# Moving 97 subtractions of a two-layer kernel from VectorE to GpSimd

## The chip, the core and the metric

The kernel runs on one core of one Trainium2 chip. The metric is the device time of the program in microseconds (us); less is better. Engines are named as the profile names them: PE is the matrix engine (TensorE), DVE the vector engine (VectorE), ACT the scalar engine (ScalarE), POOL is GpSimd, SP issues the DMA transfers. PSUM is the memory that PE writes its sums to, SBUF the working memory.

## What is computed

A chunked attention with 8 memory slots feeds two dense layers. Only the first dense layer (`_moe_ref`) matters for the change.

```python
out[:, :, c_start:c_end] = np.matmul(a, v_full)        # softmax attention, 32 queries per chunk
...
x = attention output, 3072 tokens x 512
h = np.maximum(x @ w_in, 0.0)                          # layer 1: 512 -> 2048
x = (h * h @ w_out)                                    # layer 1: 2048 -> 512
...
h = x @ w2_in                                          # layer 2
g = np.maximum(h, 0.0) + np.log1p(np.exp(-np.abs(h)))  # softplus
return (g @ w2_out)
```

The kernel keeps float32 accuracy on PE by splitting each operand into a high half, which is the value rounded to the matrix engine's format, and a low half, which is the value less its high half. A product of two such operands takes three matmuls: high by low, low by high, high by high.

## The kernel before

The 3072 tokens of layer 1 are six blocks (n = 0 to 5) of 512 tokens; a block runs 16 steps (f = 0 to 15), one for each slice of 128 of the 2048 hidden units. A step is, in PE's order:

- `h_mm(1, n, f)` (L286): 12 matmuls of 128x512 that make `hp`, one slice of x @ w_in, from the block's halves `xh`, `xl` and the weight halves `wt[1, f]`.
- `act1` (L302), on ACT: Relu into a tile `r` (L304), Square in place (L305), and a copy to `gh`, the high half (L307). It notes (gl, r, gh) in the list `rest`.
- `act1_low` (L311): takes the oldest entry of `rest` and issues gl = r - gh (L313), the low half. This is the line that the change touches.
- `out_step` (L359) with `out_mm` (L319): 12 matmuls that add gh and gl times the second weights into four PSUM banks `acc`. It stays `LOOK` = 2 steps behind `h_mm`, so PE works on other slices between the making of gh, gl and their use.

The tiles `r`, `gh` and `gl` have three buffers each. Everything up to the end of layer 1 stands under a manual schedule: each engine takes its instructions in the order in which the code issues them, and only semaphores hold them up. In the second layer only PE's order is written by hand.

Block 0 also prepares layer 1's weights. They come as 64-bit numbers by DMA, and for each slice `i` a job makes the two float32 halves: `w_a` (L98, ACT) takes the absolute value, `w_b` (L102, DVE, one input, in place) prepares the low bits, `w_d` (L107 and L110, DVE, two inputs each) joins them, `w_h` (L118, ACT) copies the high half, `w_p` (L122, DVE) subtracts for the low half. `h_mm(1, 0, f)` needs slice f's result, and `out_mm` that of its OUT part. In step f of block 0 the job of slice f + 2 runs (slice halves IN and OUT apart in the first steps), and around it the code issues:

```python
w_d(1, i, m)
w_h(1, i, m)
if k == 0:
    act1_low()
if flat:
    w_a(1, *flat[0])
    w_b(1, *flat[0])
w_p(1, i, m)
```

So DVE's queue in a step of block 0 reads L107, L110, L313, L102, L122. ACT's queue reads L304, L305, L307 (the step's `act1`), L118, then L98 of the next job. The softmax of the next block's attention stands in the same queues (`p_scores` on PE, `p_exp` and `p_norm` on DVE with L176 to L188, `p_transpose` on PE, `p_copy` on ACT at L218), and `pp` of `p_transpose` shares two PSUM buffers with `hp`. At the start of block 0 its first step is done in two halves of 256 tokens, so `rest` holds one entry more there, and L313 runs one step later than in the other blocks.

In blocks 1 to 5, `step` (L653) issues `act1_low` at the start of the step after the one that made gh. GpSimd has had six instructions in all, at the program's start.

Of the kernel before, what the change touches and what calls it, by code (L numbers as in the profile page):

```python
# [10 lines left out]
F32 = mybir.dt.float32  # L11
F32R = mybir.dt.float32r
AF = mybir.ActivationFunctionType
ALU = mybir.AluOpType
# [41 lines left out]
def body(ctx: ExitStack, tc: tile.TileContext, qk, vW, w1, w2, out):  # L56
    nc = tc.nc
# [252 lines left out]

    def act1_low():  # L311
        gl, r, gh = rest.pop(0)
        nc.vector.tensor_tensor(out=gl, in0=r, in1=gh.bitcast(F32), op=ALU.subtract)  # L313

    acc = [None] * 4
    rest = []
# [201 lines left out]
    with tc.manual_schedule(engines={mybir.EngineType.SP}):  # L518
# [20 lines left out]
        with tc.manual_schedule():  # L539
# [74 lines left out]
            for f in range(KF):  # L614
# [18 lines left out]
                for k, (i, m) in enumerate(jobs[f]):  # L633
                    flat.pop(0)
# [8 lines that stand above are left out]
                if not jobs[f]:  # L643
                    act1_low()
                if f % 4 == 0:
                    p_exp(pair)
                if f == KF - 1:
                    act1_low()
                    x_split((1, 1))
# [260 lines left out]
```

## Time and profile before

| | |
|---|---|
| time, median of 3 runs | 1107.55 us (1106.06 to 1107.64) |
| time of the profiled execution | 1106.41 us |
| its span, first to last instruction | 1104.6 us |
| PE busy | 1080.2 us, 98% |
| DVE busy | 753.2 us, 68% |
| ACT busy | 595.4 us, 54% |
| POOL busy | 0.7 us, 6 instructions |

The profiled execution lies 1.14 us under the median, and 1.81 us of its time are outside its span. PE is busy in nearly all of the span; an engine that is idle elsewhere costs nothing as long as PE doesn't wait for it. So the places to read are those in which PE waits, and what was late there.

### The profile page before, as it was taken

The numbers are of one execution on the slowest core, as the hardware profiler recorded it, in microseconds if no ns is written. First come the engines' busy times: TensorE is split into PE (matmuls) and PEld (weight loads), VectorE is DVE, ScalarE is ACT, GpSimd is POOL, SyncE is SP. The second block draws the span as 40 slices with busy tenths as digits, with TensorE's granted clock in tenths as the row PEclk, the third lists the DMA queues.
The fourth block names the chain that finished last, engine by engine and source line by source line (L and its number), as shares of the span: only waits on it lengthen the run. The fifth ranks groups of instructions, "written<-read, shape, count | busy, mean of one in ns | idle before, by whom it ended". The sixth has DMA issues, their size and how long they took to land.

```text
span 1104.6 us, 18583 instructions
## 1 busy us (share of the span) xinstructions
PE 1080.2 (98%) x7592; PEld 887.1 (80%) x7592; DVE 753.2 (68%) x1227; ACT 595.4 (54%) x926; POOL 0.7 (0%) x6
## 2 busy tenths in 40 slices
PE   6899999999999999999999999999999999999998
PEld 5678888888888888888888788888788888788886
DVE  6899586666668666777432798952798942798722
ACT  3676554454455445555544776632676632776522
POOL 0000000000000000000000000000000000000000
PEclk9899999999999999999999999999999999999999
DMA  9941253454525355442611755333555334555202
GB/s 368 408 178 45 64 166 121 150 187 154 187 88 204 105 176 177 161 153 110 225 39 64 262 186 222 117 141 137 203 188 217 111 136 147 196 200 191 77 1 76
DMA packets 49428, 174.99 MB, mean 158 GB/s; under 512 B 5312, under 2 KB 5312, under 8 KB 41152
## 3 DMA queue, kind: packets, MB, share of 16 engines
q1 hardware_dynamic: 49344, 173.82, 44.7%
q8 instruction: 59, 0.97, 0.3%
q14 instruction: 25, 0.20, 0.1%
HBM read 138.15 MB, written 35.65 MB: 157 GB/s over the span
## 4 chain that ended last, share of the span: by engine, by line
PE 91%; DVE 5%; ACT 2%; issue 1%; DMA 0%; SPq 0%; DVEq 0%
PE bk L830 23%; PE acc L328 23%; PE bk L742 18%; PE hp L292 8%; PE hp L293 7%; PE hp L294 7%; PE xs L237 1%; PE xs L156 1%; DVE cf L110 1%; DVE cf L107 1%; PE sc L156 1%; PE xp L237 1%; DVE h L753 1%; PE xpe L237 1%; ACT w L118 1%
## 5 line engine op out<-in xcount | busy, mean ns | idle before, releaser
L328 PE MATMUL acc<-gh,w 128*128 128x512 f32 (+1 forms) x776 | 238.9, 389 | 0.4 <-DVE w L122 0.4
L830 PE MATMUL bk<-ws,gh 128*128 128x512 f32 x768 | 236.6, 389 | 0.0
L742 PE MATMUL bk<-xo,ws 128*128 128x512 f32 x1008 | 231.1, 390 | 2.5 <-DVE h L791 2.5
L742 PEld LDWEIGHTS bk<-xo,ws 128*128 128x128 f32 x1008 | 188.7, 188 | 44.1 <-DVE h L791 5.1
L328 PEld LDWEIGHTS acc<-gh,w 128*128 128x128 f32 x776 | 144.0, 188 | 30.5 <-DVE w L122 0.8
L830 PEld LDWEIGHTS bk<-ws,gh 128*128 128x128 f32 x768 | 144.0, 188 | 30.1 <-ACT h L762 0.5
L292 PE MATMUL hp<-xh,w 128*128 128x512 f32 (+1 forms) x388 | 154.1, 397 | 3.5 <-ACT pt L218 3.1
L328 PE MATMUL acc<-gl,w 128*128 128x512 f32 (+1 forms) x388 | 150.5, 388 | 2.2 <-DVE gl L313 2.2
L294 PE MATMUL hp<-xh,w 128*128 128x512 f32 (+1 forms) x388 | 151.7, 391 | 0.0
L293 PE MATMUL hp<-xl,w 128*128 128x512 f32 (+1 forms) x388 | 151.6, 391 | 0.1
L830 PE MATMUL bk<-ws,gl 128*128 128x512 f32 x384 | 149.4, 389 | 0.0
L396 DVE TENSOR_TENSOR gl<-h,gh 128x512 fp32r<-128x512 f32 x96 | 66.0, 687 | 90.9 <-ACT gh L401 90.9
L401 ACT CAST gh<-h 128x512 fp32r<-128x512 f32 x96 | 59.3, 621 | 114.5 <-PE bk L830 114.2
L313 DVE TENSOR_TENSOR gl<-r,gh 128x512 fp32r<-128x512 f32 (+1 forms) x97 | 66.2, 683 | 73.0 <-ACT gh L307 72.6
L304 ACT ACTIVATE r<-hp 128x512 f32<-128x512 f32 (+1 forms) x97 | 57.2, 590 | 103.4 <-PE hp L294 99.7
L292 PEld LDWEIGHTS hp<-xh,w 128*128 128x128 f32 x388 | 73.9, 191 | 19.6 <-ACT pt L218 3.3
L328 PEld LDWEIGHTS acc<-gl,w 128*128 128x128 f32 x388 | 72.8, 188 | 17.7 <-DVE gl L313 2.9
L294 PEld LDWEIGHTS hp<-xh,w 128*128 128x128 f32 x388 | 73.8, 190 | 15.3
L293 PEld LDWEIGHTS hp<-xl,w 128*128 128x128 f32 x388 | 74.0, 191 | 14.8 <-DVE xl L282 0.3
L830 PEld LDWEIGHTS bk<-ws,gl 128*128 128x128 f32 x384 | 72.1, 188 | 15.1
L202 DVE STREAM_TRANSPOSE pt<-t 32x128 f32<-32x128 f32 x256 | 77.5, 303 | 4.3
L748 ACT ACTIVATE cf<-h 128x1024 f32<-128x1024 f32 x48 | 51.0, 1062 | 34.6 <-DVE cf L752 29.8
(81 smaller groups left out, 1139.8 us busy)
## 6 DMA issues: line engine op xcount, KB each, us to landing
ws<-wa SPq DMA_DIRECT2D x24, 1024.0 KB, 4.8
ws<-wo SPq DMA_DIRECT2D x24, 1024.0 KB, 4.8
ws<-wb SPq DMA_DIRECT2D x24, 768.0 KB, 4.3
r<-w SPq DMA_DIRECT2D x16, 1024.0 KB, 11.3
cf<-w SPq DMA_DIRECT2D x32, 512.0 KB, 5.3
qk<-qk SPq DMA_DIRECT2D x46, 336.0 KB, 5.1
v<-vW SPq DMA_DIRECT2D x44, 256.0 KB, 5.1
wo<-cf SPq DMA_DIRECT2D x16, 512.0 KB, 3.2
```

Of the source, the lines that this page charges most:

```text
L202: nc.vector.transpose(pt[b:b + 32, g], t[g * 32:(g + 1) * 32, i, h])
L292: nc.tensor.matmul(out=hp, lhsT=b, rhs=xh[:, c], start=(c == 0), stop=False)
L293: nc.tensor.matmul(out=hp, lhsT=a, rhs=xl[:, c], start=False, stop=False)
L294: nc.tensor.matmul(out=hp, lhsT=a, rhs=xh[:, c], start=False, stop=(c == KD - 1))
L304: nc.scalar.activation(out=r, in_=hp, func=AF.Relu)
L313: nc.vector.tensor_tensor(out=gl, in0=r, in1=gh.bitcast(F32), op=ALU.subtract)
L328: nc.tensor.matmul(out=acc[m][:, cols], lhsT=a, rhs=b, start=(f == 0 and j == 0 and cols.start == 0), stop=(f == KF - 1 and j == 2),)
L396: nc.vector.tensor_tensor(out=lo, in0=x, in1=hi.bitcast(F32), op=ALU.subtract)
L401: nc.scalar.copy(out=hi, in_=x)
L742: nc.tensor.matmul(out=bk, lhsT=a, rhs=b, start=(start and n == 0), stop=(n == 5), skip_group_check=not start)
L748: nc.scalar.activation(out=z, in_=h, func=AF.Abs)
L830: nc.tensor.matmul(out=bk, lhsT=a, rhs=b, start=(f == 0 and j == 0), stop=(f == KF - 1 and j == 2))
```

## The change

The subtraction of `act1_low` is issued on GpSimd's queue instead of VectorE's. Operands, tiles and its place in the code are the same.

```diff
     def act1_low():
         gl, r, gh = rest.pop(0)
-        nc.vector.tensor_tensor(out=gl, in0=r, in1=gh.bitcast(F32), op=ALU.subtract)
+        nc.gpsimd.tensor_tensor(out=gl, in0=r, in1=gh.bitcast(F32), op=ALU.subtract)
```

On DVE one instruction leaves each step. The piece below is step 2 of block 0, where the weight job of slice 4 runs (`r_4_334` is the raw slice, `w_4_741` its halves, `cf` the work tile).

```order
 L107 SCALAR_TENSOR_TENSOR cf<-cf,r_4_334 128x1024
 L110 SCALAR_TENSOR_TENSOR cf<-r_4_334,cf 128x1024
-L313 TENSOR_TENSOR gl<-r,gh 128x512
 L102 TENSOR_SCALAR r_2_186<-r_2_186 128x512
 L122 TENSOR_TENSOR w_4_741<-cf,w_4_741 128x1024
```

L102 and L122 now follow L110 directly; the other steps of layer 1 lose their L313 in the same way.

On POOL the 97 subtractions stand behind the making of the identity tile `ident`, with nothing between them. The piece is POOL's whole queue from there to the program's end.

```order
 masks.py:199 ISA
 masks.py:199 AFFINE_SELECT ident<-ident 128x128
+L313 TENSOR_TENSOR gl<-r,gh 128x256 x2
+L313 TENSOR_TENSOR gl<-r,gh 128x512 x95
 L906 UNCONDITIONAL_BRANCH
 L906 ISA
```

No other instruction shares that queue, so a subtraction can start as soon as its gh and a free gl are there.

On PE three matmuls move, where the last `out_mm` of layer 1 (`acc_5926` to `acc_5929`, slice 15) is interleaved with the first products of layer 2 (`bk`).

```order
 L328 MATMUL acc_5926<-gh,w_15_1480 128x512 x2
 L742 MATMUL bk<-xo_6081,ws 128x512
+L742 MATMUL bk<-xo_6083,ws 128x512 x3
 L328 MATMUL acc_5926<-gl,w_15_1480 128x512
 L328 MATMUL acc_5927<-gh,w_15_1480 128x512 x2
```

Three products of layer 2 now stand ahead of the first use of that slice's gl, three fewer behind the group. ACT's and SP's orders are the same.

## Rows read from the trace of the kernel before

**Rows 1.** The page: busy time, share of the span and instructions of each engine.

```profile
PE 1080.2 (98%) x7592; PEld 887.1 (80%) x7592; DVE 753.2 (68%) x1227; ACT 595.4 (54%) x926; POOL 0.7 (0%) x6
```

**Rows 2.** Windows: stretch, length, busy us: PE, PEld, DVE, ACT, POOL; clock, DMA.

```profile
30.00:72.00 42.00, 36.21 (x338) 28.40 (x337) 37.28 (x56) 26.03 (x41) 0.00 (x0) 0.92 0.90 355
72.00:125.00 53.00, 51.80 (x468) 42.13 (x469) 47.47 (x58) 37.83 (x53) 0.00 (x0) 1.00 0.18 57
...
154.00:250.00 96.00, 96.00 (x900) 78.59 (x900) 67.46 (x154) 48.47 (x87) 0.00 (x0) 1.00 0.45 153
```

**Rows 3.** PE's waits of the whole span: waiting line, releaser, us, times, longest.

```profile
PE hp L292 <- ACT pt L218: 3.1, 1, 3.1
```

**Rows 4.** The page's group of the moved line: instructions, busy us, mean ns, idle before.

```profile
L313 DVE TENSOR_TENSOR gl<-r,gh 128x512 fp32r<-128x512 f32 (+1 forms) x97 | 66.2, 683 | 73.0 <-ACT gh L307 72.6
```

**Rows 5.** Timeline of DVE, weight jobs in block 0: start, duration, instruction, [idle before].

```profile
40.85 0.42 DVE L313 TENSOR_TENSOR gl<-r,gh 128x256 fp32r<-128x256 f32 x1
41.19 0.42 DVE L102 TENSOR_SCALAR r<-r 128x512 uint32<-128x512 uint32 x1
41.62 0.69 DVE L122 TENSOR_TENSOR w<-cf,w 128x512 fp32r<-128x512 f32 x1
...
47.76 0.68 DVE L313 TENSOR_TENSOR gl<-r,gh 128x512 fp32r<-128x512 f32 x1
48.37 0.44 DVE L102 TENSOR_SCALAR r<-r 128x512 uint32<-128x512 uint32 x1
48.96 1.23 DVE L122 TENSOR_TENSOR w<-cf,w 128x1024 fp32r<-128x1024 f32 x1 [0.15 <-ACT w L118]
...
63.55 0.68 DVE L313 TENSOR_TENSOR gl<-r,gh 128x512 fp32r<-128x512 f32 x1
64.15 0.69 DVE L102 TENSOR_SCALAR r<-r 128x1024 uint32<-128x1024 uint32 x1
64.76 1.23 DVE L122 TENSOR_TENSOR w<-cf,w 128x1024 fp32r<-128x1024 f32 x1
...
73.67 1.22 DVE L122 TENSOR_TENSOR w<-cf,w 128x1024 fp32r<-128x1024 f32 x1
...
88.20 1.22 DVE L122 TENSOR_TENSOR w<-cf,w 128x1024 fp32r<-128x1024 f32 x1 [0.21 <-ACT w L118]
...
97.12 1.22 DVE L122 TENSOR_TENSOR w<-cf,w 128x1024 fp32r<-128x1024 f32 x1
...
112.75 1.22 DVE L122 TENSOR_TENSOR w<-cf,w 128x1024 fp32r<-128x1024 f32 x1 [1.32 <-ACT w L118]
...
121.38 1.22 DVE L122 TENSOR_TENSOR w<-cf,w 128x1024 fp32r<-128x1024 f32 x1 [0.52 <-ACT w L118]
```

**Rows 6.** Timeline of ACT, steps 1, 2 and 4 of block 0.

```profile
38.90 0.62 ACT L307 CAST gh<-r 128x512 fp32r<-128x512 f32 x1
40.97 0.62 ACT L118 CAST w<-cf 128x512 fp32r<-128x512 f32 x1 [1.45 <-DVE cf L110]
...
45.23 0.57 ACT L218 COPY pt<-pp 128x512 f32<-128x512 f32 x1
...
47.88 1.05 ACT L118 CAST w<-cf 128x1024 fp32r<-128x1024 f32 x1 [0.28 <-DVE cf L110]
...
63.67 1.06 ACT L118 CAST w<-cf 128x1024 fp32r<-128x1024 f32 x1 [0.75 <-DVE cf L110]
```

**Rows 7.** Timeline of PE: first gl of slice 4; first matmuls of h_mm 7, 11, 15.

```profile
73.20 0.51 PE L328 MATMUL acc<-gl,w 128*128 128x512 f32 x1 [1.82 <-DVE gl L313]
...
75.64 0.39 PE L292 MATMUL hp<-xh,w 128*128 128x512 f32 x1
...
100.20 0.39 PE L292 MATMUL hp<-xh,w 128*128 128x512 f32 x1
...
124.76 0.39 PE L292 MATMUL hp<-xh,w 128*128 128x512 f32 x1
```

**Rows 8.** Groups by line: the one instruction of POOL that reads SBUF.

```profile
masks.py:199 POOL TENSOR_SCALAR_AFFINE_SELECT ident<-ident 128x128 f32<-128x128 f32 x1 | 0.3, 292 | 0.1
```

## The prediction

> **What bounds the kernel now.** The page's busy times come first: PE is busy for 98% of the span, DVE for 68%, POOL for nothing [rows 1]. So nothing that only unloads DVE can help, except where PE waits for DVE. The windows show where that is. From 154 to 250 us PE is busy for all of its 96 us, while DVE has 28.5 us to spare. From 30 to 72 us PE is idle for 5.8 us and DVE is busy for 37.3 of 42 [rows 2]. That is block 0, where DVE and ACT make the weight halves. PE's waits name its longest hold there: 3.1 us for the copy pt (L218) on ACT [rows 3]. A second one, 1.82 us at 73.20, is for gl of slice 4, the very instruction that moves [rows 7]. So the timelines of DVE, ACT and PE in block 0 decide the case.
>
> What the reader is to see in DVE's timeline is what L122, the last instruction of a weight job, waits for. It needs L118 on ACT, and L118 needs DVE's L110. In step 2, L118 ends at 47.88 + 1.05 = 48.93 [rows 6] and L122 starts at 48.96; L313 and L102 lie in between, and 0.15 us are idle all the same [rows 5]. Step 1 ends L118 at 41.59 and starts L122 at 41.62, step 4 at 64.73 and 64.76 [rows 5, 6]. **L313 stands in the time that DVE spends on ACT's copy anyway.**
>
> **The change, part by part.** *What it removes.* 97 instructions of 683 ns, 66.2 us of DVE [rows 4]. In blocks 1 to 5 that is time which PE doesn't wait for: nothing. In block 0 each L313 is covered by L118, so L122 can't start sooner: nothing again. The pt copy stays too: it stands behind ACT's L118 and L98, which follow L110, not L313. What goes is the wait of 1.82 us, since POOL can make gl(4) right behind its gh instead of one job later. But what comes next is late as well. The weights of slice 7 are ready at 73.67 + 1.22 = 74.89 [rows 5], and h_mm(7), which needs them, starts at 75.64 [rows 7]. Of the 1.82 us only 0.75 can be had.
>
> *What it adds.* 97 instructions on POOL, alone in their queue, and a semaphore between POOL and PE in place of DVE's. ACT's `r` tiles are now freed by POOL; with three buffers that is no hold. The three matmuls that PE's order moves at the end of layer 1 are the same work: nothing.
>
> *How long one takes.* The trace has no two-input subtraction on POOL. The nearest row is a one-input one, 292 ns for 128 elements [rows 8]. Taking 0.1 us of that as fixed, 1.5 ns an element is left; 512 elements then take 0.87 us for one stream, and 1.64 us if the second stream costs as much again. My estimate lies between, 1.2 us. The Trainium skill (GPSIMD Engine Reference, 3.1 Elementwise — side-by-side cycle accounting) gives 4497 ns for 2048 elements; a quarter, 1.12 us, is an estimate from that page, and the sum below would be 0.9 us smaller by it.
>
> *What the overlap costs DVE.* The trace has no moment with both engines at work on SBUF, so this cost is bounded: nothing, or DVE stands still for POOL's whole instruction. A hint lies in the widths. The one-input L102 takes 0.69 us for 1024 elements, the two-input L122 takes 1.23 [rows 5]: a DVE instruction with two inputs uses all that DVE can read, one with one input reads at twice the pace and so uses it too. L107, L110, L102 and L122 are all of these kinds. If POOL reads through a path of DVE's, they and POOL exclude each other. I take that end as likelier, because these instructions leave no reading unused. The rule stands in the Trainium skill (SBUF — State Buffer, Who interferes with whom): a DVE instruction with two SBUF inputs, or in a two-port mode, and a GpSimd instruction that reads SBUF hold each other up until the first has finished. By that rule the time is the sum below, without it the first rival's 1106.85; no row here shows it.
>
> *The sum, if they exclude each other.* DVE runs L110 and L102 back to back, and POOL gets its turn in the pause ahead of L122. L102 issues where L313 did.
> - Step 1: gh is ready at 39.52 [rows 6]. L102 ends at 40.85 + 0.42 = 41.27, POOL at 42.47; L122 was at 41.62: **0.85 us** later.
> - Step 2: L102 ends at 48.20, POOL at 49.40, L122 was at 48.96: **0.44**. Step 3 has the same rows, with 0.03 more room: **0.4**.
> - Step 4: L102 is wide; it ends at 63.55 + 0.69 = 64.24, POOL at 65.44, L122 was at 64.76: **0.68**. Step 5 repeats this.
>
> Together 3.05 us. L122 feeds the next job's instructions, so the delay adds up. Slice 7's weights come at 74.89 + 3.05 = 77.94, and h_mm(7) starts then instead of at 75.64: PE is **2.3 us** late. Steps 6, 7 and 9 repeat step 4 (0.68 each); in step 8 L122 had waited 0.21 us for ACT, so 0.47. That makes 5.56 at L122 of slice 11: 97.12 + 1.22 + 5.56 = 103.90, where h_mm(11) was at 100.20 [rows 5, 7]: PE is now **3.7 us** late. Steps 10 and 11 add 0.68 each. Step 12 had 1.32 us of waiting for ACT, so it gives back 0.64; step 13 has no L102, and POOL's 1.2 us exceed L118's 1.06 by 0.14. The total is 6.42, and slice 15's weights come at 121.38 + 1.22 + 6.42 = 129.02, where h_mm(15) was at 124.76: **4.3 us** late at the end of block 0. From there PE has no wait to lose or win, and it keeps the 4.3 us to the end. The profiled execution of 1106.41 us becomes 1110.7; the median of the runs stands 1.14 us above it, so on that scale the forecast is 1111.8 us.
>
> With POOL at 0.87 us the same steps cost 0.52, 0.11, 0.07, 0.35, 0.35 and then 0.35 a step; slices 7, 11 and 15 then hold PE by some 0.7 us, 1108.3. With 1.64 us, 1.1 a step, it is some 10 us, 1117.5.
>
> **The rivals.**
>
> *No price for overlap* (chance 0.28). POOL and DVE read side by side. For it speaks that no row shows the opposite. Then gl(4) is early, h_mm(7) starts at 74.94, and PE gains 0.7 us: 1106.85. That is on the other side of before, by one mechanism, the wait at 73.20, and it decides wherever POOL costs DVE less than the room in front of L122 (0.35 us from 41.27, 0.76 us from 48.20). More than 2 us it can't give, since the wait itself has only 1.82.
>
> *Half a price* (0.10): POOL near 0.87 us, or a sharing that slows both a little. Some 0.7 us lost, 1108.3.
>
> *POOL is served first* (0.15). It takes its turn between L107 and L110 where gh is ready by then, in steps 1, 5, 9 and 13, and ahead of L102 elsewhere. A turn ahead of L110 costs the full 1.2 us, one ahead of L102 some 0.5 to 0.7. Slices 7, 11 and 15 then come 4.1, 7.2 and 8.9 us later, less the room of 0.75, 1.86 and 2.16 that PE had in front of them: 6.7 us lost, 1114.3.
>
> *POOL comes too late* (0.02). DVE's back-to-back work leaves it no turn, and PE waits for gl. Against it: gh(1) is ready at 39.52 and its gl was begun by DVE at 47.76 [rows 5, 6] without a hold of PE, so each POOL instruction has some 9 us. It decides only from there, and would cost several us a step.
>
> **How the numbers follow.** Forecast 0.45, the rivals 0.28, 0.10, 0.15 and 0.02. A difference of 0.2%, 2.2 us, is about what a measurement of this kernel can tell from no change. Slower by more: forecast, served first, too late, 0.62. Within: half a price and most of the first rival, 0.34. Faster by more: 0.04, the rest of the first rival, if something that I take as covered isn't. The likeliest time is 1111.8. The range goes down to the first rival's 1106.9 and up to 1115.5, past the served-first case; left out are the slowest POOL and a little below.
>
> **What would show it.** Right: POOL busy for some 1.2 us in each of 97 instructions, DVE's L122 in block 0 with waits on something that isn't ACT, or its instructions lengthened where POOL runs; h_mm(7) near 78, h_mm(11) near 104, h_mm(15) near 129 us, and no wait of PE for gl. Blocks 1 to 5 keep their length (PE 96 of 96 us), whatever DVE does. Wrong: DVE's instructions keep their 0.69 and 1.23 us beside a busy POOL and h_mm(7) starts at 75, or PE waits in blocks 1 to 5.

## Result, and the profile of the changed kernel

The changed kernel takes 1115.14 us (median of 6 runs, 1113.51 to 1116.75), the kernel before 1107.45 us (6 runs, 1106.06 to 1107.64). The ratio is 1.0070, with an interval of 1.0057 to 1.0083: 6.3 to 9.2 us slower. The forecast was 1111.8 us, slower, in a range of 1106.9 to 1115.5 us. The direction was right and the time lies in the range, near its upper end: a loss of 4.3 us was expected, and it is 7.7 us. The profiled execution of the changed kernel took 1115.76 us, with a span of 1114.0 us.

The page's busy times and its group of the moved line answer to [rows 1] and [rows 4]:

```profile
PE 1084.6 (97%) x7592; PEld 889.6 (80%) x7592; DVE 737.6 (66%) x1130; ACT 595.1 (53%) x926; POOL 132.6 (12%) x103
...
L313 POOL TENSOR_TENSOR gl<-r,gh 128x512 fp32r<-128x512 f32 (+1 forms) x97 | 131.9, 1359 | 478.1 <-ACT gh L307 443.5
```

DVE has lost 97 instructions, which took 66.2 us, but only 15.6 us of its busy time (753.2 to 737.6). So DVE's other instructions have become longer by some 50 us. That is the first sign of a price for the overlap.

The windows, with the stretches of [rows 2] and one more (stretch, length, busy us of PE, PEld, DVE, ACT, POOL; clock, DMA):

```profile
30.00:72.00 42.00, 35.49 (x337) 28.73 (x336) 35.93 (x46) 24.61 (x39) 7.25 (x5) 0.89 0.90 349
72.00:125.00 53.00, 49.30 (x449) 39.34 (x448) 48.63 (x50) 35.90 (x51) 14.20 (x8) 0.97 0.19 62
154.00:250.00 96.00, 96.00 (x900) 78.90 (x899) 62.90 (x137) 48.24 (x86) 20.90 (x16) 1.00 0.44 152
440.00:535.00 95.00, 93.32 (x822) 75.50 (x821) 60.61 (x118) 46.36 (x84) 19.67 (x16) 1.00 0.40 136
```

The last stretch in before:

```profile
440.00:535.00 95.00, 95.00 (x835) 78.28 (x834) 64.12 (x133) 50.69 (x91) 0.00 (x0) 1.00 0.46 153
```

PE now loses time in two places. One is block 0, as forecast. The other is at 440 to 535 us, where PE is busy for 93.32 of 95 us (in before for all 95); nothing was expected there. From 154 to 250 us it is busy for all of 96 us, as before.

PE's waits of the whole span (waiting line, releaser, us, times, longest), to be read beside [rows 3]:

```profile
PE hp L292 <- ACT pt L218: 7.2, 2, 4.7
...
PE hp L292 <- ACT xh L267: 0.7, 1, 0.7
PE acc L328 <- POOL gl L313: 0.7, 1, 0.7
```

The wait for pt was 3.1 us in one place and is 7.2 us in two. The wait of 1.82 us for gl(4) at 73.20 [rows 7] is gone. The waits for xh of L267 and for POOL's gl are new; both stand where block 4 ends.

In block 0, DVE's timeline in steps 1, 2 and 5 (start, duration, instruction, [idle before]) reads, to be set beside [rows 5]:

```profile
41.09 0.68 DVE L107 SCALAR_TENSOR_TENSOR cf<-cf,r 128x512 uint32<-128x512 uint32 x1
41.81 1.66 DVE L110 SCALAR_TENSOR_TENSOR cf<-r,cf 128x512 uint32<-128x512 uint32 x1
43.39 0.42 DVE L102 TENSOR_SCALAR r<-r 128x512 uint32<-128x512 uint32 x1
44.16 0.69 DVE L122 TENSOR_TENSOR w<-cf,w 128x512 fp32r<-128x512 f32 x1 [0.35 <-ACT w L118]
...
49.15 1.22 DVE L110 SCALAR_TENSOR_TENSOR cf<-r,cf 128x1024 uint32<-128x1024 uint32 x1
50.29 1.56 DVE L102 TENSOR_SCALAR r<-r 128x512 uint32<-128x512 uint32 x1
51.76 1.21 DVE L122 TENSOR_TENSOR w<-cf,w 128x1024 fp32r<-128x1024 f32 x1
...
74.81 2.21 DVE L110 SCALAR_TENSOR_TENSOR cf<-r,cf 128x1024 uint32<-128x1024 uint32 x1
76.94 0.68 DVE L102 TENSOR_SCALAR r<-r 128x1024 uint32<-128x1024 uint32 x1
78.13 1.23 DVE L122 TENSOR_TENSOR w<-cf,w 128x1024 fp32r<-128x1024 f32 x1 [0.51 <-ACT w L118]
```

In before, the L110 of step 1 reads:

```profile
40.24 0.69 DVE L110 SCALAR_TENSOR_TENSOR cf<-r,cf 128x512 uint32<-128x512 uint32 x1
```

POOL's timeline of the changed kernel in the same steps:

```profile
41.17 1.75 POOL L313 TENSOR_TENSOR gl<-r,gh 128x512 fp32r<-128x512 f32 x1 [7.12 <-ACT gh L307]
50.27 1.29 POOL L313 TENSOR_TENSOR gl<-r,gh 128x512 fp32r<-128x512 f32 x1 [7.35 <-ACT gh L307]
...
73.68 2.25 POOL L313 TENSOR_TENSOR gl<-r,gh 128x512 fp32r<-128x512 f32 x1 [5.89 <-ACT gh L307]
```

The timelines of the changed kernel are read together. In step 1 POOL's instruction is begun at 41.17, while DVE runs L107 until 41.77. DVE's L110 is begun at 41.81 and lasts 1.66 us in place of 0.69; POOL ends at 42.92, and L110 0.55 us behind that, at 43.47. So POOL waited for L107 to end, then ran for 1.15 us, and L110 stood still meanwhile. In step 2, L110 ends as POOL begins, POOL takes 1.29 us, and it is L102 that lasts 1.56 us instead of 0.44. Step 5 is like step 1, L110 lasting 2.21 us instead of 1.23. **In these steps POOL gets its turn as soon as the running DVE instruction ends**, ahead of the next one in DVE's queue.

PE's timeline: the first matmuls of h_mm 7, 11 and 15, to be set beside [rows 7]:

```profile
79.65 0.62 PE L292 MATMUL hp<-xh,w 128*128 128x512 f32 x1 [2.48 <-ACT pt L218]
...
105.97 0.40 PE L292 MATMUL hp<-xh,w 128*128 128x512 f32 x1
...
130.87 0.47 PE L292 MATMUL hp<-xh,w 128*128 128x512 f32 x1 [0.16 <-DVE w L122]
```

They stand 4.0, 5.8 and 6.1 us later than before. One caution on reading such a difference: TensorE's granted clock in block 0, as a mean over its levels of 2.4 GHz (1.00) and 1.2 GHz, is not the same in every execution. A kernel in which nothing of block 0 is changed (only one step of block 4, below) had its h_mm(7) at 79.92, with a granted clock of 0.71 from 25 to 32 us, where before had 1.00. So the sizes below come from medians of several runs wherever there are several, and single profiles are used for mechanisms and for stretches in which the clock is 1.00. The profile of before is also an early one: in the seven other profiles in which block 0 is as in before, h_mm(7) starts at 76.4 to 79.9 us and h_mm(15) at 126.0 to 129.1.

### The profile page after: what moved, and what is told of

The parts are those of the page before. It is cut to its first block, busy times and chain, and to the rows that moved or that the text cites. A ratio compares the mean times of both kernels' runs of the same rounds, so it can differ in the third digit from the quotient of the medians.

```text
span 1114.0 us, 18702 instructions
## 1 busy us (share of the span) xinstructions
PE 1084.6 (97%) x7592; PEld 889.6 (80%) x7592; DVE 737.6 (66%) x1130; ACT 595.1 (53%) x926; POOL 132.6 (12%) x103
## 4 chain that ended last, share of the span: by engine, by line
PE 49%; DVE 3%; ACT 1%; issue 0%; DVEq 0%
PE bk L830 23%; PE bk L742 18%; PE acc L328 4%; PE hp L294 1%; PE hp L293 1%; PE hp L292 1%; DVE h L753 1%; DVE cf L751 0%; DVE h L791 0%; DVE gl L396 0%; DVE cf L752 0%; ACT cf L749 0%; ACT cf L748 0%; ACT cf L750 0%; DVE xl L268 0%
## 5 line engine op out<-in xcount | busy, mean ns | idle before, releaser
L313 POOL TENSOR_TENSOR gl<-r,gh 128x512 fp32r<-128x512 f32 (+1 forms) x97 | 131.9, 1359 | 478.1 <-ACT gh L307 443.5
L396 DVE TENSOR_TENSOR gl<-h,gh 128x512 fp32r<-128x512 f32 x96 | 66.0, 688 | 90.7 <-ACT gh L401 90.7
L401 ACT CAST gh<-h 128x512 fp32r<-128x512 f32 x96 | 59.3, 621 | 114.2 <-PE bk L830 113.9
```

The lines of the kernel that those rows point to most:

```text
L313: nc.gpsimd.tensor_tensor(out=gl, in0=r, in1=gh.bitcast(F32), op=ALU.subtract)
L396: nc.vector.tensor_tensor(out=lo, in0=x, in1=hi.bitcast(F32), op=ALU.subtract)
L401: nc.scalar.copy(out=hi, in_=x)
```

## The experiments

Two theories stood against each other for the price: **exclusion** (POOL's reads and DVE's two-input or fast one-input instructions hold each other up) and **dependence** (PE waits for POOL's slower gl). Where the loss lies was open as well: in block 0 alone, or also in the blocks in which PE was never idle before. All kernels are made from the kernel before or after by the edit shown; `n` is the block, kept with the entry of `rest`. Their line numbers are one or two higher behind an added line (L313 may read L314).

### Block 0 and the others apart

```diff
-        nc.gpsimd.tensor_tensor(out=gl, in0=r, in1=gh.bitcast(F32), op=ALU.subtract)
+        engine = nc.gpsimd if n > 0 else nc.vector
+        engine.tensor_tensor(out=gl, in0=r, in1=gh.bitcast(F32), op=ALU.subtract)
```

> The subtraction is on GpSimd in blocks 1 to 5 only (80 of the 97); block 0 keeps it on VectorE. Theory (a GpSimd subtraction and VectorE's two-input instructions exclude each other, and it is block 0's weight jobs that pay for it): block 0 as before, h_mm of slice 7 at 75.6 and of slice 15 at 124.8 us; what is left is the cost of the late blocks, where the profile of the changed kernel lost 3.2 of its 9.35 us: 0 to 3 us over before. Rival (each subtraction is slow or late on GpSimd, and PE waits for gl): 80 of 97 instructions stay, so most of the loss stays, 6 us or more, with waits of PE for GpSimd in the trace.

Measured: 1111.84 us against 1108.0, a ratio of 1.0030 (1.0020 to 1.0039), 3.3 us slower, by the median a little above the expected 3. The second kernel has `n == 0` for the condition:

> The subtraction is on GpSimd in block 0 only (17 of the 97). Theory: 4 to 7 us over before, with L110 or L102 beside a GpSimd instruction 1 us longer than its 0.69 or 1.23 us, and h_mm of slice 15 some 6 us late. Rival (slow or late subtractions everywhere): at most 1 us over before.

Measured: 1111.49 us, 1.0027 (1.0016 to 1.0039), 3.0 us slower, less than the 4 to 7 us expected. Each half of the change costs some 3 us. Their sum, 6.3 us, agrees with the change's 7.7 us within the intervals. PE's timeline of the kernel with block 0 alone, first matmuls of h_mm 7, 11 and 15:

```profile
78.50 0.50 PE L292 MATMUL hp<-xh,w 128*128 128x512 f32 x1 [2.48 <-ACT pt L218]
...
104.79 0.40 PE L292 MATMUL hp<-xh,w 128*128 128x512 f32 x1
...
129.72 0.47 PE L292 MATMUL hp<-xh,w 128*128 128x512 f32 x1 [0.19 <-DVE w L122]
```

The prediction had put them near 78, 104 and 129, but kernels with block 0 unchanged come nearly as late (above), so these times don't show its mechanism. The waits do. PE's wait for the pt copy ahead of h_mm(3), 3.1 us in before, is 4.7 us in both kernels: that copy follows step 1's L110 through ACT's queue, and L110 is held for 0.97 us. The second wait, 2.48 us ahead of h_mm(7), is new, and the 1.82 us for gl(4) are saved. In before the pt copy ahead of h_mm(7), on ACT, is

```profile
74.58 0.57 ACT L218 COPY pt<-pp 128x512 f32<-128x512 f32 x1
```

which ends at 75.15 us, later than slice 7's weights; so it does in this kernel (78.44 against 78.20 us). Behind the wait of 2.48 us the clock fell, in this profile and in that of the changed kernel. In the windows of the kernel with block 0 alone this is the row:

```profile
79.00:84.00 5.00, 5.00 (x75) 3.70 (x74) 4.97 (x5) 4.15 (x6) 1.35 (x1) 0.66 0.00 0
```

The step from h_mm(7) to h_mm(8) takes 8.46 us in it and 6.74 in before, at 1.00: 1.7 us more. That delay of PE swallows a part of what DVE loses later, so it isn't added to the delay of slice 11: h_mm(11) has no wait, and h_mm(15) has one of 0.19 us. Nor is it a cost of the change alone. In five of the seven other kernels with block 0 as in before, the granted clock from 75 to 80 us was 0.66 to 0.70 too, behind the wait of 1.8 us for gl(4); one of them, which moves only a step of block 4, reads:

```profile
75.00:80.00 5.00, 3.83 (x11) 3.08 (x12) 4.97 (x6) 4.35 (x6) 0.00 (x0) 0.66 0.00 0
```

### Overlap without dependence

DVE makes gl as before. POOL does the same subtraction once more behind it, into `r`, which nobody reads afterwards.

```diff
         nc.vector.tensor_tensor(out=gl, in0=r, in1=gh.bitcast(F32), op=ALU.subtract)
+        nc.gpsimd.tensor_tensor(out=r, in0=r, in1=gh.bitcast(F32), op=ALU.subtract)
```

> VectorE makes gl as before; behind each, GpSimd subtracts once more, r - gh into r itself, which nobody reads. So GpSimd does the same work, but no result of layer 1 waits for it; only ACT's reuse of r, two steps later, does. Theory (exclusion): VectorE's L102 or L122 in block 0 is held by up to 1.15 us where GpSimd runs, and the kernel is 3 to 8 us slower than before. Rival (the loss comes from waiting for GpSimd's result): as before within 1 us, VectorE's instructions keep their durations.

Measured: 1116.04 us against 1108.0, 1.0069 (1.0052 to 1.0086), 7.6 us slower, and PE never waits for POOL. Timelines of this kernel in step 2, DVE and then POOL:

```profile
48.63 0.68 DVE L313 TENSOR_TENSOR gl<-r,gh 128x512 fp32r<-128x512 f32 x1
49.23 0.42 DVE L102 TENSOR_SCALAR r<-r 128x512 uint32<-128x512 uint32 x1
49.83 2.05 DVE L122 TENSOR_TENSOR w<-cf,w 128x1024 fp32r<-128x1024 f32 x1 [0.17 <-ACT w L118]
```

```profile
49.46 1.34 POOL L314 TENSOR_TENSOR r<-r,gh 128x512 f32<-128x512 f32 x1 [6.82 <-DVE gl L313]
```

POOL ends at 50.80, L122 1.08 us behind that: 2.05 us instead of 1.23. So nothing has to wait for POOL's result for a loss to arise; the overlap alone makes one as large as the change's. It isn't in the same places, though. At the end of block 4 this profile loses nothing, and in block 0 more (h_mm(7) 5.6 us late): here POOL holds L122, the end of the weight job, DVE's own L313 is still there, and PE's waits for DVE's gl grow from 2.2 us in all to 4.9. So the agreement of the two totals is no evidence by itself.

### Writing without reading

POOL fills gl with zeros twice before DVE's subtraction, so it is busy but reads nothing.

```diff
+        for _ in range(2):
+            nc.gpsimd.memset(gl.bitcast(F32), 0.0)
```

> VectorE makes gl as before; ahead of that, GpSimd sets each gl to zero twice, so it writes SBUF for some 1 us a step and reads nothing. Theory that the two exclude each other over reading: VectorE's two-input instructions (L107, L110, L122) keep 0.69 and 1.23 us beside GpSimd, at most the one-input L102 is held; within 2 us of before. Rival (any GpSimd instruction on SBUF holds VectorE): L107, L110 or L122 longer by up to the length of GpSimd's instruction, 3 to 7 us over before.

Measured: 1107.83 us against 1108.0, 1.0002 (0.9993 to 1.0011): no difference. The page has POOL busy for 102.8 us in 194 such instructions. Timelines of this kernel, POOL and then DVE:

```profile
43.01 1.11 POOL L308 MEMSET gl<- 128x512 f32 x2 [4.22 <-PE acc L330]
```

```profile
43.12 0.69 DVE L110 SCALAR_TENSOR_TENSOR cf<-r,cf 128x512 uint32<-128x512 uint32 x1
43.73 0.94 DVE L102 TENSOR_SCALAR r<-r 128x1024 uint32<-128x1024 uint32 x1
44.59 0.67 DVE L122 TENSOR_TENSOR w<-cf,w 128x512 fp32r<-128x512 f32 x1
```

The two-input L110 keeps its 0.69 us under a writing POOL. The one-input L102, which runs at twice the pace, is held for 0.25 us (0.94 in place of 0.69), and that is covered. So it is POOL's reads that hold the two-input instructions.

### One input instead of two

As in the kernel without dependence, but POOL copies gh into `r`.

```diff
         nc.vector.tensor_tensor(out=gl, in0=r, in1=gh.bitcast(F32), op=ALU.subtract)
+        nc.gpsimd.tensor_copy(r, gh.bitcast(F32))
```

> As e3, but GpSimd's extra instruction is a one-input copy, gh into r (nobody reads it), in place of the second subtraction. If what excludes is that GpSimd reads SBUF at all: L122 is held for the length of that copy, by the memset's rate some 0.5 to 0.9 us, and the kernel loses a good half of e3's 8 us, 3 to 6. If only a second input stream excludes: as before within 1 us, L122 keeps 0.69 and 1.23 us.

Measured: 1109.91 us against 1107.7, 1.0019 (1.0007 to 1.0032), 2.1 us slower: by the median less than the 3 to 6 us of the first expectation, more than the 1 us of the second. Timelines of this kernel in step 4, POOL and then DVE:

```profile
64.84 0.92 POOL L314 COPY r<-gh 128x512 f32<-128x512 f32 x1 [7.38 <-DVE gl L313]
```

```profile
65.20 1.63 DVE L122 TENSOR_TENSOR w<-cf,w 128x1024 fp32r<-128x1024 f32 x1
```

POOL ends at 65.76, L122 again 1.07 us behind it. So a second input stream isn't needed for POOL to hold DVE. The copy takes 0.65 us in step 3 and 0.61 at the shortest, about half of the subtraction's 1.29. DVE's busy time grows by 16.3 us over before, against 50.4 us under the second subtraction; that is less than half, which is not explained here. The profiled execution of this kernel (1107.42 us) was 2.5 us under its median, so the place of the loss is not read from it.

### Served in the pause

The forecast had POOL served in DVE's pause ahead of L122. This kernel forces that in block 0 and leaves the other blocks on DVE: `act1_low` stands behind `w_b`, with a small instruction of DVE on the same tile ahead of it, so that POOL can't begin sooner.

```diff
-                    if k == 0:
-                        act1_low()
                     if flat:
                         w_a(1, *flat[0])
                         w_b(1, *flat[0])
+                    if k == 0:
+                        nc.vector.memset(rest[0][0][:, 0:1].bitcast(F32), 0.0)
+                        act1_low()
                     w_p(1, i, m)
```

> Block 0 only, as e2, but GpSimd is made to come in where the prediction put it: VectorE sets one column of gl to zero behind L102, and the subtraction waits for that, so it begins in VectorE's pause ahead of L122. Theory (a turn costs about the same wherever it is taken, since VectorE has no idle time to give beyond what L118 already takes): L110 and L102 keep 1.23 and 0.69 us, L122 is held by 0.6 to 0.9 us in each step, the weights of slice 7 come 3 to 3.6 us late as in e2 (4.3 there), and the kernel is 3 to 6 us slower than before. Rival (being served ahead of L110 is what costs): the loss falls to less than half of e2's 3.5 us.

Measured: 1114.17 us against 1107.7, 1.0064 (1.0047 to 1.0080), 7.1 us slower, where block 0 alone lost 3.0, and more than both expectations. Timelines in step 2, POOL, DVE, and PE's longest wait for gl:

```profile
50.87 1.28 POOL L314 TENSOR_TENSOR gl<-r,gh 128x512 fp32r<-128x512 f32 x1 [6.60 <-DVE gl L643]
```

```profile
51.46 1.78 DVE L122 TENSOR_TENSOR w<-cf,w 128x1024 fp32r<-128x1024 f32 x1 [0.76 <-ACT w L118]
```

```profile
69.31 0.80 PE L329 MATMUL acc<-gl,w 128*128 128x512 f32 x1 [2.77 <-POOL gl L314]
```

L122 ends 0.55 us later than its 1.23 would have it; over steps 2 to 5 it is 0.55, 0.51, 0.78 and 0.83. The forecast priced them at 0.44, 0.4, 0.68 and 0.68 with a POOL instruction of 1.2 us: its pricing of the pause is right to 0.15 us a step. In the changed kernel the same four steps cost 0.27, 0.22, 0.50 and 0.97, less in sum (1.96 against 2.67 us). Step 1, where a turn ahead of L110 costs 0.97 us, nearly levels that. But in the pause gl itself comes too late: PE waits for it 5 times, 7.0 us in all. Early service is the cheaper of the two mainly for that.

### Where in blocks 1 to 5

Only block 4 on POOL (`n == 4`), and all blocks but 0 and 4 (`n in (1, 2, 3, 5)`):

> The subtraction is on GpSimd in block 4 only (16 of the 97). Theory: all that e1 lost behind block 0 was lost at one place, the end of block 4, where VectorE's late L389 and L396 delay a store, the load behind it, and the ACT instructions queued behind that load's first reader: 3 us over before, block 0 as before, h_mm of the first two slices of block 5 together 3 us late. Rival (a little in every late block): under 1 us over before.

Measured: 1110.14 us against 1107.7, 1.0026 (1.0014 to 1.0037), 2.9 us slower.

> The complement: on GpSimd in blocks 1, 2, 3 and 5 (64 of the 97). Theory: VectorE's instructions are held there as well, but PE has nothing to wait for: within 0.7 us of before. Rival (every subtraction on GpSimd costs): two thirds of the 7.7 us, or at least 2.5.

Measured: 1108.24 us, 1.0010 (1.0000 to 1.0020). So by the medians block 4 makes most of the 3.3 us; to the other four blocks the interval leaves 0 to 2.2 us.

The next four kernels ran once each. They move chosen steps of block 4 only, with the block and step kept in `rest`, for instance:

```diff
+        engine = nc.gpsimd if nf in ((4, 9), (4, 10)) else nc.vector
```

> Only the subtractions of steps 9 and 10 of block 4 run on POOL, the two that held DVE's L386 and L396 in the kernel with block 4 alone. Read as growth of PE's delay between the first matmul of step 15 of block 4 and the second step of block 5 within this profile (2.4 us where all of block 4 is on POOL). Theory 'chain': the held VectorE instructions delay a store, the load queued behind it and the casts behind that load, so these two steps alone cost 1 to 2 us. Rival 'last gl': the loss comes from PE waiting for the late gl of step 15, so 0 here.

> Only the subtraction of step 13 of block 4 runs on POOL, which held DVE's L385 for 1.1 us shortly before the casts of block 5's x. Chain: 0.5 to 1.2 us of growth at the end of block 4. Last gl: 0.

> Steps 9, 10 and 13 of block 4 on POOL. Chain: the sum of the two runs before, 1.5 to 2.4 us, nearly all that block 4 alone loses. Last gl: 0.

> Block 4 on POOL without steps 9, 10 and 13. Chain: 0 to 0.5 us of growth at the end of block 4. Last gl: all of the 2.4 us, since step 15 is still on POOL.

Measured, as growth of PE's delay against before at the end of block 4 (from the first matmul of its step 15 to that of the second step of block 5): 0.17, 0.00, 0.31 and 0.00 us. (Their single times, 1108.16, 1110.62, 1109.90 and 1110.43 us beside one of 1108.75 for before, say nothing at this size.) **Both theories missed.** No selected step carries the loss, and the sum over parts is far from the 2.38 us of block 4 as a whole. The reason is seen in one number of each profile, the lateness of a cast: how long after the first matmul of step 15 of block 4 ACT begins the cast `xh` (L267), which the first step of block 5 needs. In before the two rows are, ACT and then PE:

```profile
513.04 2.17 ACT L267 CAST xh<-xf 128x512 fp32r<-128x512 f32 x4
```

```profile
508.43 0.50 PE L292 MATMUL hp<-xh,w 128*128 128x512 f32 x1
```

that is 4.61 us. In the kernel with block 4 alone, ACT and then PE:

```profile
517.87 2.16 ACT L267 CAST xh<-xf 128x512 fp32r<-128x512 f32 x4
```

```profile
509.60 0.50 PE L292 MATMUL hp<-xh,w 128*128 128x512 f32 x1
...
518.53 0.50 PE L292 MATMUL hp<-xh,w 128*128 128x512 f32 x1 [0.47 <-ACT xh L267]
```

that is 8.27 us. Read in the same way in ten kernels (the other four lie at 4.84 to 5.52 us, with 0.01 to 0.09):

| POOL has | cast xh begins after, us | PE's delay grows, us |
|---|---|---|
| nothing (before) | 4.61 | 0 |
| block 4 without steps 9, 10, 13 | 4.56 | 0.00 |
| blocks 1, 2, 3, 5 | 4.64 | 0.01 |
| a second subtraction, all blocks | 5.12 | 0.01 |
| step 13 of block 4 | 5.45 | 0.00 |
| steps 9 and 10 | 5.92 | 0.17 |
| steps 9, 10 and 13 | 6.02 | 0.31 |
| block 4 | 8.27 | 2.38 |
| all (after) | 8.92 | 3.03 |
| blocks 1 to 5 | 9.06 | 3.18 |

Up to some 5.8 us PE doesn't feel it; above that every us of lateness costs a us. So blocks 1 to 5 have a margin, some 1.2 us at this place, and not an unlimited one. In ACT's timeline of the changed kernel it is seen what stands ahead of the cast:

```profile
502.42 0.66 ACT L381 ACTIVATE cf<-cf 128x512 f32<-128x512 f32 x1 [4.68 <-DMA cf<-w]
...
523.06 0.66 ACT L381 ACTIVATE cf<-cf 128x512 f32<-128x512 f32 x1 [3.00 <-DMA cf<-w]
523.63 2.16 ACT L267 CAST xh<-xf 128x512 fp32r<-128x512 f32 x4
```

L381 prepares second-layer weights, and it waits for a load (L376), which in SP's queue stands behind a store of weights that DVE has finished with L396. DVE's row in the changed kernel that comes before the first of the two stores is one of those that POOL holds:

```profile
494.58 1.42 DVE L396 TENSOR_TENSOR cf<-cf 128x512 fp32r<-128x512 f32 x1 [0.91 <-ACT cf L401]
```

In before the same two rows, DVE and then ACT, are

```profile
486.09 0.68 DVE L396 TENSOR_TENSOR cf<-cf 128x512 fp32r<-128x512 f32 x1
```

```profile
493.02 0.66 ACT L381 ACTIVATE cf<-cf 128x512 f32<-128x512 f32 x1 [1.47 <-DMA cf<-w]
```

From the end of L396 to L381 it is 6.42 us in the changed kernel, 6.25 in before and 6.26 with block 4 alone, so nearly all of the lateness is there before the store. So DVE's delay goes through SP's queue to ACT's queue, and by the cast behind it to PE. In PE's timeline of the changed kernel it arrives as:

```profile
524.28 0.51 PE L292 MATMUL hp<-xh,w 128*128 128x512 f32 x1 [0.72 <-ACT xh L267]
525.01 0.50 PE L293 MATMUL hp<-xl,w 128*128 128x512 f32 x1 [0.22 <-DVE xl L268]
...
529.07 0.51 PE L328 MATMUL acc<-gl,w 128*128 128x512 f32 x1 [0.68 <-POOL gl L313]
```

The waits add up to 1.62 us, the delay to 3.03: the first matmul behind each wait starts over with a longer row (0.5 us in place of 0.39), and the starts of its neighbours move with it; the rest is not accounted for. The wait of 0.68 us for POOL's gl belongs to the same chain, since ACT made that gh late, behind the cast. A weight load of PE, at 520.99, also waits 0.48 us for POOL's gl; there ACT made gh late too, behind a cast (L401) that waited 3.26 us for DVE, whose L385 POOL had held (1.54 us).

How the steps of block 4 together make 3.66 us of lateness, when steps 9, 10 and 13 make 1.41 and the rest none, is seen in part. In step 13 both kernels lose 1.1 us (L385 takes 1.55 and 1.56 us, in before 0.43). With all of block 4 on POOL, DVE comes to step 9 already 0.9 us late, with three only 0.1. In step 9 the later gh then makes POOL hold L386 (1.59 us, in before 0.69), where with three steps POOL began before L385 and held only that one (0.70, in before 0.43): 0.7 us more in steps 9 and 10. And from L396 to L381 the first store and load took 6.3 us with all of block 4 and 5.7 with three steps. So parts of it depend on where POOL's turns fall, and the loads' own time differs too; why the early steps give 0.9 us in one kernel and 0.1 in that with the rest of block 4 stays open.

## Why the prediction came out as it did

- **What bounds the kernel.** Right for block 0: the loss is made where PE waits, by the weight jobs and what follows them in ACT's queue. The reading that nothing can be lost elsewhere, because PE is busy for all of its 96 us there, was wrong (below).
- **What the removal gives.** Right in kind. The wait for gl(4) went [rows 7] and brought nothing, since the pt copy and slice 7's weights came later: h_mm(7) waits 2.48 us for them. The forecast had "the pt copy stays"; that was wrong, as L110 itself is held and the copy with it (the wait of 3.1 us became 4.7). It also left out that the pt copy ahead of h_mm(7) ended at 75.15 us in before, behind the weights' 74.89, so the room in front of h_mm(7) was 0.5 us, not 0.75.
- **POOL and DVE exclude each other.** Right, and shown: POOL's reads lengthen DVE's rows, overlap without dependence costs the kernel time, writing without reading costs nothing that could be measured. The rule of the Trainium skill (SBUF — State Buffer, Who interferes with whom) is borne out here, in its difference between reading and only writing too: L110 0.69 us under the memset, 1.66 us under the subtraction. The rival "no price" (1106.85 us) falls.
- **How long POOL takes.** The estimate of 1.2 us is near: 1.28 to 1.29 us where it isn't held. The mean of 1359 ns on the page contains waiting, up to 2.25 us in one row. The estimate from the Trainium skill (GPSIMD Engine Reference, 3.1 Elementwise — side-by-side cycle accounting), 1.12 us, is too short by 0.17 us for this size; it would have made the sum smaller by 1.0 us, not 0.9, since 13 steps each change by 0.08. The bounds of 0.87 and 1.64 us were built on a poor neighbour [rows 8]: one stream takes 0.61 to 0.65 us, two take 1.29.
- **Where POOL is served.** Wrong. The forecast let DVE run L110 and L102 back to back and put POOL into the pause; in fact POOL takes its turn at the end of whatever DVE instruction is running when gh is ready. The rival "served first" had the places right (ahead of L110 in steps 1, 5, 9 and 13, ahead of L102 elsewhere; only in step 8 did POOL run in the pause) and their price too high: a turn ahead of L110 costs 0.97 us at L122, not 1.2, one ahead of a narrow L102 0.22 to 0.27, ahead of a wide one 0.50. Up to step 5 the sum is 0.97 + 0.27 + 0.22 + 0.50 + 0.97 = 2.93 us, where the forecast, by other places, had 3.05. The total agreed by chance, the places didn't.
- **Block 0's loss.** Forecast 4.3 us; block 0 alone measures 3.0 us (1.8 to 4.3). That its h_mm(7), (11) and (15) stand at 78.5, 104.8 and 129.7 us, where 78, 104 and 129 were named, is in part luck, since block 0 unchanged reached 79.9 and 129.1 in one profile. The route was different: PE was held by the pt copies, which the forecast had left out, and only in second place by slice 7's weights; in this profile the clock behind that wait took 1.7 us at once, and DVE's later delays hid behind that.
- **"From there PE has no wait to lose or win."** This is the step that failed, and it makes the distance to the result: the term was put at 0, and 3.3 us (2.2 to 4.3) are lost in blocks 1 to 5, most of it where block 4 ends. The sign that the prediction itself had named for being wrong, "PE waits in blocks 1 to 5", is there. The 28.5 us of spare DVE time from 154 to 250 us [rows 2] said nothing about it: at the end of block 4 what counts is the order of ACT's queue, in which a cast that PE needs stands behind an instruction that waits for a load.
- **No wait of PE for gl.** One of 0.68 us came, and one of 0.48 us of a weight load, in that same place. The rival "POOL comes too late" isn't borne out by them, since ACT made both gh late; POOL's longer run (1.29 us in place of 0.68) adds to them.
- **The rivals' times.** "Served first" gave 1114.3 us, the nearest to 1115.14, but with all of its 6.7 us in block 0, where about half is lost; that nearness is chance.

## What to carry to other kernels

An instruction that was moved here from VectorE to GpSimd was not gone from VectorE: where it read SBUF beside two-input or fast one-input VectorE instructions, it held them while it ran, and it ran for 1.29 us where VectorE needed 0.68. So ask first what VectorE has in its queue at that moment, not how busy it is on average. And where an engine is busy for all of a stretch, look up how late each of its inputs could still come (here 1.2 us for a cast) before calling a delay free.

## What the runs showed of the hardware that was not expected

- When DVE's instructions stand back to back, a waiting POOL instruction still gets its turn as soon as the running one ends. In the changed kernel this holds in steps 1, 2 and 5 of block 0, as shown above; L110 or L102 then lasts about 1 us longer.
- A held DVE instruction is shown as running in the trace: its row grows (0.69 to 1.66 us), and idle time doesn't. A held two-input instruction ends at a nearly fixed distance behind POOL's end in the steps read: 0.55 us for 512 elements, 1.07 to 1.09 us for 1024. For the one-input L102 of step 2, with 512 elements, it is 0.29 us.
- A memset on POOL left a two-input DVE instruction alone (0.69 us) and held a fast one-input one by 0.25 us.
- POOL's rows grow in the same way while DVE holds it, from 1.29 up to 2.25 us, so a mean over the page's group is no price of the instruction.
